# One more quarter by seven products, and the first slice of w_in as float32 through SyncE's queue

## The chip, the cores and the metric

The kernel runs on one NeuronCore of one Trainium2 chip. The metric is the device time of one execution in microseconds (us). The kernel before took 203.43 us in the median of three runs (203.06 to 203.89).

## What is computed

First a linear attention with decay, then a two-layer perceptron with exact GELU on its output. Inputs are float32; q, k and v are [4, 8, 768, 64] (batch, heads, sequence, head width), w_in is [512, 2048] and w_out [2048, 512]; the output is [3072, 512] float32.

```python
for b in range(nb):                       # blocks of 64 positions, S = 768
    intra = (qb @ kb.T) * Dmask[None]     # Dmask: lam ** (i - j) for i >= j, else 0
    out[:, :, sl] = intra @ vb + (qb * lam_pow[None]) @ kv_state
    kv_state = lam_block * kv_state + (kb * rev_pow[None]).T @ vb
x = out.transpose(0, 2, 1, 3).reshape(B * S, H * D)      # [3072, 512]
h = x @ w_in
g = 0.5 * h * (1.0 + erf(h / sqrt(2)))
return g @ w_out
```

## The kernel before

**Tiling.** The sequence is cut into six groups of 128 positions (g = 0 to 5). A group is 128 positions of each of the four batches, so 512 tokens, and is done in two pairs of batches (p = 0, 1). For each group and pair the kernel loads q, k and v, transposes q and k on TensorE (groups 0 to 2) or by DMA (3 to 5), computes scores (`sc` or `u`), masks them on VectorE (`m`), adds to the state (`ka`, `kb`, or within `u` and `ii`), computes the attention output (`o`, `oo`) and writes the scaled result `x` on VectorE. Group 0 goes another way than the rest (`add_paired`, L465): two neighbouring positions lie side by side, scores use four PSUM banks and need four masks, and each scaling of v is one instruction of 128x512.

**The first product** (x times w_in, then GELU) is cut into four quarters of 512 columns of d_ff, c = 0 to 3, in each group. A quarter is computed in one of two ways. The plain one (`add_mm1_half`, L653) has for both pairs two halves H g.j.p with j = 2c and 2c+1, each of 8 matmuls of 128x256 and one GELU on ScalarE: 32 matmuls for a quarter. The other (`add_mm1_quads`, L734) splits the product two by two and uses seven products instead of eight, h g.c.1 to h g.c.7, of 4 matmuls of 128x256 each: 28 matmuls, with two copies (`hm`, `hs`), two adds on VectorE (`ha` L777, `hb` L782) and four GELUs. It needs sums of the slices of x (`X`, once for a group) and of w_in (`V`, once for all groups). STD lists the quarters done the plain way: all of group 0, and quarters 0 and 2 of group 1. The second product (`P`, `add_mm2`) works by seven products throughout, with sums `S` of GELU outputs and `W` of w_out.

**Loads.** q, k, v and both weights are cast from float32 to bfloat16 by the DMA, which GpSimd issues (`nc.gpsimd.dma_start`; L345 for group 0, L356, L317 and L320 for the rest, L369 for w_in, L374 for w_out). w_in comes in four slices of 512 columns: ld.wi0, ld.wi4, ld.wi8, ld.wi12. SyncE's queue carries the load of lam, the DMA transposes and the stores. GpSimd also scales v (`vh`) where the order says so, and it works through its loads and its scalings in one line: a scaling that waits for its v holds up all loads behind it.

**The order.** The instructions of all engines are written out by hand-placed names in the string ORDER (L26 to L76). `Program.emit` prints them in that order, each on its engine; a name may carry another engine behind a slash (`vh000/POOL`). Steps called idleN are dummy matmuls that keep TensorE's clock up; `idleN/SP` means that this one is left out. Costs that stand with the operations are stored and not used when the program is printed. Each engine works strictly in its order, and semaphores are derived from the tiles that an operation reads and writes.

The head of the order, before (cut):

```
ld.wi4 ld.q00 iota ld.k00 ld.v00 tb0 ... ldlam ... ln cols tix tw tpa tid tmp ... Tq00 idle11 Tk00
ld.q01 ld.k01 ld.wi0 xp Ek000/DVE vh001 vh000/POOL ... sc00 ka00 ld.v01 ld.q10 ld.k10 ld.v10 ...
o00 x000 x001 Eq010 Eq011 Ek010 Ek011 H0.0.0a H0.0.0b sc01 idle16 ... H0.3.0a ... vh010/POOL m0101 m0100 m0111
ld.wi8 ld.k11 ld.wi12 vh011 m0110 Tq10 H0.1.0a H0.1.0b ka01 Tk10 kb01 o01 H0.2.0a H0.3.0b H0.2.0b ...
ld.q11 vh101 vh100 ld.v11 Eq100 Eq101 Ek101 Ek100 sa01 ks10 x011 x010 ... u10 sm10 tmk m101 m100 H0.4.0 H0.5.0
```

`ld.q00` is q of group 0 and pair 0; `Tq00` its transpose, `Ek000` the copy of a transposed half from PSUM; `vh000` a scaling of half of v; `H0.0.0a` the first half of the tokens of H0.0.0. Matmuls of all kinds have line L452 in the profile (a helper), transposes L435 and L437, plain copies L300 (ScalarE) and L302 (VectorE).

The functions that the change touches, and what calls them:

Of the kernel before, what the change touches and what calls it, by code (L numbers as in the profile page):

```python
# [26 lines left out]
ld.wi4 ld.q00 iota ld.k00 ld.v00 tb0 idle0/SP ldlam idle1/SP idle2/SP idle3/SP idle4/SP idle5/SP idle6/SP ln cols tix  # L27
tw tpa tid tmp idle7/SP idle8/SP idle9/SP idle10/SP Tq00 idle11 Tk00 ld.q01 ld.k01 ld.wi0 xp Ek000/DVE vh001
vh000/POOL xx xw xc Eq001 Eq000 Ek001 idle12/SP idle13/SP idle14/SP idle15/SP bits sc00 ka00 ld.v01 ld.q10 ld.k10
ld.v10 kb00 m0000 m0011 m0010 m0001 Tq01 Tk01 o00 x000 x001 Eq010 Eq011 Ek010 Ek011 H0.0.0a H0.0.0b sc01 idle16  # L30
idle17/SP idle18/SP idle19/SP idle20/SP idle21/SP idle22/SP idle23/SP H0.3.0a sa00/ACT xv gtab g0.0.0 V0.0 vh010/POOL
m0101 m0100 m0111 ld.wi8 ld.k11 ld.wi12 vh011 m0110 Tq10 H0.1.0a H0.1.0b ka01 Tk10 kb01 o01 H0.2.0a H0.3.0b H0.2.0b
ld.q11 vh101 vh100 ld.v11 Eq100 Eq101 Ek101 Ek100 sa01 ks10 x011 x010 g0.1.0 g0.2.0 u10 sm10 tmk m101 m100
H0.4.0 H0.5.0 i10 g0.4.0 g0.5.0 Tk11 H0.0.1 sa10 Ek110/DVE Ek111/DVE V0.2 V1.0 ks11/DVE g0.3.0 H0.7.0 H0.6.0 g0.0.1
g0.7.0 g0.6.0 H0.2.1 Tq11 o10 Eq110/DVE x101 x100 g0.2.1 Eq111 vh110/ACT H0.1.1 H0.3.1 ld.v20 ld.wo00 ld.k20 vh111 u11
g0.1.1 g0.3.1 sm11 H0.5.1 H0.4.1 V2.1 m111 m110 S0.0.0 V3.0 S1.0.0 V1.2 i11 o11 x110 x111 X0.1 X1.1 vh200/ACT g0.5.1
H1.1.0 H0.6.1 vh201/ACT g1.1.0 g0.4.1 sa11/ACT g0.6.1 H1.0.1 H0.7.1 h1.1.1 H1.0.0 g0.7.1 g1.0.0 g1.0.1 S2.0.0 X2.1
ks20/DVE ld.q21 ld.q20 ld.wo10 Tq20 Tk20 W0.0 S0.0.4 Ek200/DVE Eq201 h1.1.5 hm1.1/DVE Eq200 Ek201/DVE X3.1 W1.0 H1.5.0
H1.4.0 hs1.1 u20 g1.5.0 h1.1.6 h1.1.2 H1.5.1 H1.4.1 m200 m201 sm20 ii20 g1.1.00 g1.5.1 ha1.1 h1.1.3 fe20 g1.4.1 g1.4.0
oo20 h1.1.7 h1.3.5 h1.3.1 H1.1.1 ld.k21 ld.v21 ld.wo01 ld.v31 g1.1.01 vh211/ACT vh210 ld.wo11 ld.q40 ld.k40 V3.2 sa20  # L40
x200 ks21/DVE hb1.1 h1.1.4 P1.0a x201 S1.0.4 g1.1.11 g1.1.10 g1.1.1 P1.0b hs1.3 hm1.3 W0.2 P5.0a P5.0b h1.3.6 h1.3.2
pm.0 ps.0 ld.v30 ld.q30 ld.k30 ld.q31 ld.k31 ld.v40 V2.2 V2.3 S3.0.0 W1.2 W2.2 V2.0 Tq21 S3.0.4 Eq211/DVE ha1.3 Tk21
P6.0a P6.0b h1.3.7 P2.0a g1.3.00 Eq210 W2.0 S0.1.0 hb1.3 Ek210 Ek211 u21 m211 m210 vh300/ACT h1.3.3 P2.0b sm21 h2.0.1
c11.0 vh301/ACT g1.3.01 S2.0.4 pa.0 W3.2 ii21 h1.3.4 fe21 oo21 g1.3.10 g1.3.11 vh310/ACT P3.0a P3.0b P7.0a P7.0b x211
x210 X0.2 X1.2 W3.0 hs2.0 h2.0.2 h2.0.5 c12.0 hm2.0 g2.0.00 sa21/ACT c22.0 S0.1.4 X2.2 h2.0.6 ha2.0 P4.0a P4.0b h2.1.1
Tq30 Tk30 h2.0.7 ks30 S2.1.4 X3.2 hb2.0 h2.0.3 g2.0.01 u30 h2.0.4 P1.1a c21.0/DVE m300 h2.1.5 P5.1a m301 g2.0.10 sm30
vh311 ii30 hs2.1 S1.1.4 fe30/POOL Tq31 st0.11 Tk31 st0.10 Tk40 st0.01 st0.00 Tq40 h2.1.6 P5.1b oo30 hm2.1 ha2.1 h2.1.3
P1.1b h2.1.7 h2.1.2 vh401 sa30/ACT S3.1.4 ks31/DVE x301 x300 u31 pm.1 g2.0.11 hb2.1 h2.1.4 ps.1 S1.1.0 g2.1.01 g2.1.00
h2.2.1 h2.2.5 g2.1.10 m310 S2.1.0 m311 hs2.2 hm2.2/DVE sm31 g2.1.11 P6.1a h2.2.6 P2.1a h2.2.2 ii31 ha2.2 h2.2.7
fe31/POOL oo31 h2.2.3 g2.2.00 hb2.2 sa31/ACT ld.v41 ld.v50 ld.q41 ld.k41 ld.q51 ld.v51 ld.q50 g2.2.01 h2.3.1 h2.2.4  # L50
P2.1b h2.3.5 P6.1b x311 S3.1.0 x310 vh400/DVE hm2.3/DVE g2.2.10 hs2.3 c11.1 ks40 h2.3.6 ha2.3 h2.3.2 u40 h2.3.3 h2.3.7
g2.3.00 X0.3 pa.1 g2.2.11 g2.3.01 m400 X1.3 X2.3 hb2.3 g2.3.11 S2.2.4 m401 sm40/DVE S0.2.4 P3.1a P3.1b h3.0.5 h2.3.4
h3.0.1 P7.1a P7.1b c22.1 hm3.0 g2.3.10 hs3.0 ii40 h3.0.6 ha3.0 c12.1/DVE vh411 X3.3 P4.1a h3.0.2 h3.0.7 h3.0.3
sa40/ACT g3.0.00 g3.0.01 hb3.0 P4.1b h3.1.5 c21.1/DVE S0.2.0 g3.0.11 h3.0.4 h3.1.1 P1.2a g3.0.10 hs3.1 P5.2a h3.1.6
hm3.1 S1.2.4 vh410 S1.2.0 h3.1.2 g3.1.00 st1.01 st1.00 Tk41 Tq41 fe40 st1.11 Tq50 oo40 P5.2b ha3.1 h3.1.7 h3.1.3 x400
hb3.1 x401 S3.2.0 pm.2/DVE ks41 g3.1.01 h3.2.1 P1.2b h3.1.4 h3.2.5 u41 ps.2/DVE P2.2a g3.1.11 g3.1.10 hs3.2 sm41
h3.2.6 hm3.2 m410 m411 P2.2b ii41 h3.2.2 g3.2.00 ha3.2 h3.2.7 hb3.2 fe41/POOL h3.2.3 h3.3.1 oo41 h3.2.4 g3.2.01 h3.3.5
P6.2a g3.2.10 hs3.3 c11.2 hm3.3 g3.2.11 vh500/DVE h3.3.6 P6.2b h3.3.2 vh501 S0.3.0 x410 x411 S3.2.4 ha3.3 h3.3.7 X0.4
pa.2 hb3.3 S1.3.0 X1.4 S3.3.0 S2.2.0 h3.3.3 g3.3.00 P3.2a h3.3.4 h4.0.1 g3.3.11 g3.3.01 h4.0.5 P3.2b P7.2a g3.3.10
hs4.0 h4.0.6 P7.2b h4.0.2 c12.2/DVE X2.4 sa41 hm4.0 ha4.0 X3.4 g4.0.00 h4.0.7 hb4.0 S2.3.4 ks50/DVE c22.2 S0.3.4  # L60
ld.k51 ld.k50 Tk50 st2.00 st1.10 Tq51 Tk51 P1.3a h4.0.3 h4.0.4 h4.1.1 g4.0.01 g4.0.10 h4.1.5 hm4.1 hs4.1 u50 P4.2a
h4.1.6 sm50 h4.1.2 P4.2b g4.1.00 m501 ha4.1 m500 S2.3.0 h4.1.7 h4.2.1 h4.1.3 ks51 g4.0.11 ii50 g4.1.01 hb4.1 S1.3.4
c21.2/DVE vh510 fe50/POOL vh511 h4.1.4 g4.1.10 oo50 hs4.2/DVE h4.2.5 P5.3a x500 x501 hm4.2/DVE P5.3b h4.2.6 u51 ha4.2
h4.2.2 g4.1.11 sm51/DVE h4.2.3 h4.2.7 P1.3b m510 m511 ii51 hb4.2 fe51/POOL st2.10 st2.11 st2.01 g4.2.01 g4.2.00 h4.3.1
pm.3 ps.3/DVE h4.2.4 oo51 g4.2.10 hs4.3 P2.3a h4.3.6 h4.3.5 P6.3a P2.3b g4.2.11 c11.3 x510 x511 hm4.3/DVE ha4.3 h4.3.7
hb4.3 X0.5 h4.3.2 P6.3b S3.3.4 pa.3 g4.3.00 h4.3.3 h4.3.4 h5.0.1 P7.3a P7.3b g4.3.01 g4.3.11 g4.3.10 hs5.0 h5.0.2
h5.0.5 g5.0.00 hm5.0 X1.5 S0.4.4 h5.0.6 X2.5 c22.3 P4.3a P4.3b ha5.0 h5.0.7 h5.0.3 S1.4.4 hb5.0 X3.5 S3.4.4 g5.0.01
P3.3a h5.0.4 h5.1.1 h5.1.5 P3.3b g5.0.10 hs5.1 h5.1.6 hm5.1 g5.0.11 c21.3/DVE S0.4.0 ha5.1 P5.4a h5.1.2 g5.1.00 h5.1.7
S2.4.0 c12.3/DVE hb5.1 S1.4.0 h5.1.3 P5.4b h5.2.1 g5.1.01 h5.1.4 h5.2.5 P1.4a pm.4 g5.1.11 g5.1.10 P1.4b hs5.2/DVE
h5.2.6 hm5.2 ps.4 st3.11 st3.00 st3.10 st3.01 h5.2.2 P6.4a ha5.2 g5.2.00 S0.5.0 h5.2.7 h5.2.3 g5.2.01 hb5.2 P2.4a  # L70
h5.2.4 h5.3.1 P2.4b P6.4b g5.2.11 g5.2.10 c11.4 S0.5.4 S2.4.4 hs5.3/DVE h5.3.6 h5.3.2 h5.3.5 g5.3.00 hm5.3 S1.5.0 pa.4
ha5.3 S3.4.0 P7.4a P7.4b h5.3.7 P3.4a P3.4b S1.5.4 hb5.3 S3.5.0 c22.4 c12.4 h5.3.3 h5.3.4 P4.4a P4.4b S2.5.4 S2.5.0
g5.3.11 g5.3.10 g5.3.01 S0.5.6 S1.5.6 c21.4/DVE S2.5.6 P1.5a P1.5b ps.5 P5.5a P5.5b P6.5a P6.5b pm.5 S3.5.4 st4.01
st4.00 st4.10 st4.11 S3.5.6 pa.5 P2.5a P2.5b c11.5/DVE P7.5a st5.00 P7.5b P3.5a c22.5 P4.5a c12.5a/DVE c21.5a/DVE
P3.5b P4.5b c12.5b c21.5b st5.11 st5.01a st5.10a st5.01b st5.10b
# [66 lines left out]
def kernel(  # L142
# [155 lines left out]
    def copy(eng, dst, src):  # L298
        if eng == "ACT":
            nc.scalar.copy(dst, src)  # L300
        else:
            ENG[eng].tensor_copy(dst, src)  # L302
# [63 lines left out]

    def add_w_in(kf0, kf1):
        f = slice(kf0 * 128, kf1 * 128)
        add("ld.wi%d" % kf0, "POOL", lambda: nc.gpsimd.dma_start(w_in[:, :, f], w_in_r[:, :, f]), (),  # L369
            ["wi%d.%d" % (kf, kh) for kf in range(kf0, kf1) for kh in range(2)], ("w", kf1 - kf0))  # L370

# [625 lines left out]
```

## Time and profile before

| | before |
|---|---|
| median of 3 runs | 203.43 us |
| the profiled execution's own time | 204.17 us |
| span of its instructions | 202.3 us |
| TensorE (PE) busy | 186.3 us, 92% |
| VectorE (DVE) busy | 141.6 us, 70% |
| ScalarE (ACT) busy | 115.4 us, 57% |
| GpSimd (POOL) busy | 82.6 us, 41% |
| mean granted TensorE clock | 0.983 |

How to read it: the time of the profiled execution is the span and 1.87 us around it, and is itself 0.74 us above the median of the runs. In a list of waits a row gives who waited, for what, the sum, the number of waits and the longest. In a timeline a row gives start, duration, engine, line, operation, what was written from what, a count and in brackets the idle time before it with its releaser. In a table of stretches each engine's busy time stands with its count of instructions, then the granted clock, the DMA engines' share and what they moved in GB/s (bytes as written, so for casting loads the bfloat16 bytes). Matmuls are pipelined: a group's busy time, not the mean of one, gives what a matmul costs in a stream.

### The profile page before, as it was taken

How to read it: one execution, taken by the hardware profiler on the slowest of the kernel's cores; microseconds unless marked ns; L12 is line 12 of the kernel's file. 1: busy time of each engine (PE TensorE's matmuls, PEld its weight loads, DVE VectorE, ACT ScalarE, POOL GpSimd, SP SyncE). 2: the span in 40 equal slices, each digit the busy share in tenths (PEclk: the TensorE clock that was granted, in tenths of full speed). 3: DMA queues.
4: the chain of work that ended last, by engine and by line, in shares of the span. 5: the costliest groups of instructions: out<-in, count | busy, mean ns of one | idle time of the engine just before them, and what ended most of it. 6: DMA issues, size and time to landing. Idle time of an engine off the chain costs nothing.

```text
span 202.3 us, 6864 instructions
## 1 busy us (share of the span) xinstructions
PE 186.3 (92%) x2971; PEld 160.0 (79%) x2972; DVE 141.6 (70%) x255; ACT 115.4 (57%) x239; POOL 82.6 (41%) x112
## 2 busy tenths in 40 slices
...
GB/s 53 182 187 174 141 188 159 180 164 166 143 162 151 132 155 190 232 33 21 102 156 214 170 29 52 55 236 26 158 4 0 78 81 52 3 0 104 107 72 139
DMA packets 92398, 23.52 MB, mean 116 GB/s; under 512 B 82128, under 2 KB 92368, under 8 KB 92368
## 3 DMA queue, kind: packets, MB, share of 16 engines
...
q1 hardware_dynamic: 19376, 9.44, 21.0%
...
## 4 chain that ended last, share of the span: by engine, by line
PE 86%; DMA 7%; POOL 3%; DVE 2%; issue 1%; ACT 0%; POOLq 0%; ACTq 0%; DVEq 0%
PE M L452 37%; PE N L452 36%; PE X L452 9%; DMA qr<-in_q_dram 4%; DMA vr<-in_v_dram 3%; PE KV L452 2%; PE N L437 1%; POOL vr L345 1%; PE X L437 1%; POOL qr L345 1%; POOL kr L345 1%; POOL vh L403 1%; POOL w_in L369 0%; DVE N L302 0%; DVE m L782 0%
## 5 line engine op out<-in xcount | busy, mean ns | idle before, releaser
L452 PEld LDWEIGHTS <-w_in 128*128 128x128 bf16 x512 | 47.4, 100 | 7.1 <-issue 0.7
L763 ACT ACTIVATE g<-M 128x512 bf16<-128x512 f32 x51 | 29.7, 596 | 33.1 <-PE M L452 31.7
L452 PE MATMUL M<-x,w_in 128*128 128x256 bf16 (+1 forms) x360 | 45.1, 270 | 1.0 <-DVE x L525 0.9
L452 PEld LDWEIGHTS <-S 128*128 128x128 bf16 x384 | 37.3, 98 | 4.6
L452 PEld LDWEIGHTS <-g 128*128 128x128 bf16 x288 | 28.0, 98 | 3.5
L414 POOL TENSOR_TENSOR vh<-vr,lam_w 128x256 bf16<-128x256 bf16 x16 | 9.9, 663 | 39.5 <-PE X L452 39.4
L452 PE MATMUL N<-w_out,g 128*128 128x256 bf16 x192 | 24.2, 273 | 0.1
L452 PEld LDWEIGHTS <-V 128*128 128x128 bf16 x216 | 20.3, 98 | 2.9 <-issue 0.2
L452 PE MATMUL N<-T,S 128*128 128x256 bf16 x176 | 22.2, 273 | 0.0
L452 PE MATMUL N<-w_out,S 128*128 128x256 bf16 x176 | 21.2, 273 | 0.0
L452 PE MATMUL M<-xs,w_in 128*128 128x256 bf16 x136 | 20.5, 273 | 0.0
L452 PE MATMUL M<-xs,V 128*128 128x256 bf16 x136 | 19.9, 273 | 0.0
L777 DVE TENSOR_TENSOR M<-m,M 128x512 f32<-128x512 f32 x17 | 11.8, 694 | 10.2 <-PE M L452 7.8
L686 DVE TENSOR_TENSOR S<-g 128x1024 bf16<-128x1024 bf16 (+1 forms) x26 | 16.6, 643 | 2.2 <-ACT g L763 2.2
L668 ACT ACTIVATE g<-M 128x512 bf16<-128x512 f32 x24 | 13.8, 595 | 6.4 <-PE M L452 6.3
L782 DVE TENSOR_TENSOR m<-m,M 128x512 f32<-128x512 f32 x17 | 11.6, 685 | 7.8 <-PE M L452 7.6
L588 DVE TENSOR_TENSOR scm<-X,mask 128x512 bf16<-128x512 f32 x20 | 13.1, 685 | 3.4 <-PE KV L452 3.2
L634 DVE TENSOR_TENSOR x<-X,lam_x 128x512 bf16<-128x512 f32 x20 | 13.1, 684 | 1.7 <-PE X L452 1.6
L452 PE MATMUL KV<-vh,kr 64*64 64x64 bf16 x352 | 13.5, 200 | 0.2
L763 ACT ACTIVATE g<-m 128x512 bf16<-128x512 f32 x18 | 11.4, 631 | 3.1 <-DVE m L782 3.1
L356 POOL DMA_DIRECT2D qr<-in_q_dram x10 | 12.0, 1200 | 0.0
L452 PE MATMUL N<-T,g 128*128 128x256 bf16 x96 | 12.0, 273 | 0.0
...
## 6 DMA issues: line engine op xcount, KB each, us to landing
...
```

What stands on the lines that cost most here:

```text
L345: nc.gpsimd.dma_start(to[half(c)].rearrange("i (h e) -> i h e", h=H), bass.AP(src.tensor, src.offset + (2 * p + c) * H * S * D + g * C * D ...
L356: add("ld.%s%d%d%s" % (n, g, p, suffix(cs)), "POOL", lambda: nc.gpsimd.dma_start(dst, source(n, g, p, cs)), (), rkeys(n, g, p, cs), ("load ...
L414: ENG[e].tensor_mul(o_[:, c, h0:h1], v_[:, c, h0:h1], tab[:, h0:h1, None].to_broadcast((128, h1 - h0, D)))
L437: nc.tensor.transpose(b16[:, c], r_[:, c], ident)
L452: return nc.tensor.matmul(*a, skip_group_check=True, **kw)
L588: add(name("m", hi), "DVE", lambda hi=hi: nc.vector.tensor_mul(m_[:, hi, cr], sc[hi][:, cr], mask[:, None, None, :].to_broadcast((128, nc_ ...
L634: add(name("x", bl), "DVE", lambda bl=bl: nc.vector.tensor_mul(x_[:, cr, :, half(bl)], o[bl][:, cr], lam_x[:, None, :, half(bl)].to_broadc ...
L668: lambda: nc.scalar.activation(gt[g % 2][:, 2 * j:2 * j + 2, t], seen(bk, "n t", n=2), ACT.Gelu),
L686: lambda i=i, op=op, l=l, r=r: nc.vector.tensor_tensor(s(i)[0], l[0], r[0], op), l[1] + r[1], s(i)[1],
L763: lambda: nc.scalar.activation(gt[g % 2][:, 4 * c + fo:4 * c + 3 + fo:2, th * 2 * C:(th + 1) * 2 * C], src, ACT.Gelu),
L777: add("ha" + nm, "DVE", lambda: nc.vector.tensor_add(seen(bc, "q t", q=2), f5, seen(bb, "q t", q=2)), [bb, k5], [bc], ("ps", 512))
L782: add("hb" + nm, "DVE", lambda: nc.vector.tensor_add(f7, f5, seen(bb, "q t", q=2)), [bb, k5], [k7], ("ps", 512))
```

## The change

It has three parts. Quarter 2 of group 1's first product leaves STD, so it is done by seven products. The slice ld.wi0 of w_in (columns 0 to 511) is no longer cast by a DMA of GpSimd: SyncE's queue loads it as float32 in two transfers (ld.wi0a, ld.wi0b, half of the rows of w_in each, 512 KB each) into the four output staging tiles `osb`, which hold nothing yet, and four copies of 128x512 (cw00, cw01, cw10, cw11) cast it into the w_in tile, three on ScalarE and one on VectorE. And the whole order is new.

```diff
-STD = ((0, 0), (0, 1), (0, 2), (0, 3), (1, 0), (1, 2))
+STD = ((0, 0), (0, 1), (0, 2), (0, 3), (1, 0))
...
+HWI = (0,)
...
     def add_w_in(kf0, kf1):
         f = slice(kf0 * 128, kf1 * 128)
+        if kf0 in HWI:
+            for kh in range(2):
+                ks = slice(2 * kh, 2 * kh + 2)
+                add("ld.wi%d%s" % (kf0, "ab"[kh]), "SP", lambda ks=ks: nc.sync.dma_start(
+                    osb[:, ks].rearrange("p k z e -> p k (z e)"), w_in_r[:, ks, f]), (),
+                    over(["o%d" % (2 * kh), "o%d" % (2 * kh + 1)]), ("hloadw", 1))
+                for z in range(2):
+                    fz = slice((kf0 + 2 * z) * 128, (kf0 + 2 * z + 2) * 128)
+                    add("cw%d%d" % (kh, z), "ACT|DVE|POOL", lambda e, ks=ks, z=z, fz=fz: copy(
+                        e, w_in[:, ks, fz], osb[:, ks, z, :]), ["o%d.%d" % (2 * kh + k_, z) for k_ in range(2)],
+                        ["wi%d.%d" % (kf0 + 2 * z + y, kh) for y in range(2)], ("cv", 512))
+            return
         add("ld.wi%d" % kf0, "POOL", lambda: nc.gpsimd.dma_start(w_in[:, :, f], w_in_r[:, :, f]), (),
```

The head of the new order (cut):

```
iota ld.q00 ld.wi0a ldlam ln tw tpa tmp ld.k00 cols tb0 tid xp cw01 cw00 ld.wi0b cw10/DVE tix ... ld.v00 ...
idle12 Tq00 bits ... Tk00 idle18 Ek000/DVE Eq001 Eq000 Ek001 sc00 vh000 vh001 ka00 ld.q01 ld.k01
ld.v01 ld.wi4 ld.q10 m0011 m0010 m0000 m0001 Tq01 kb00 Tk01 o00 idle19 ... ld.k10
ld.v10 ld.wi8 vh010/POOL ld.k11 vh011/POOL ld.wi12 xx xw Ek010/DVE x000 cw11 xv xc sa00/ACT Ek011 gtab x001 Eq011/DVE
Eq010/DVE H0.0.0a sc01 H0.1.0a H0.0.0b H0.3.0a m0101 tmk m0111 m0110 m0100 g0.0.0 H0.1.0b Tq10 H0.2.0a V0.0 ka01 kb01
o01 Tk10 H0.2.0b H0.3.0b g0.1.0 sa01/ACT Ek101/DVE x011 Eq100/DVE x010 Eq101/DVE vh100 ks10 Ek100 g0.2.0 H0.5.0 ld.q11
vh101 ld.v11 ld.q20 ld.v20 ld.k20 u10 g0.3.0 sm10 Tk11 H0.4.0 ...
```

Steps whose engine changes up to the scores of group 2's second pair (u21): vh000, vh110, vh201 and vh210 go to VectorE, vh011 from VectorE to GpSimd; Ek010, Eq010, Eq011, Ek101, Eq100, Eq101, hm1.2 and pm.0 are on VectorE in the new order, Ek110, Ek200, Ek201, Eq110, hm1.1, ks11, ks20, ks21, sa01 and sa20 no longer are. Of the dummy matmuls idle12 (two), idle18 and idle19 (one each) are printed; before it was idle11 (two) and idle16 (one). The order of the second half and of the end is new in detail too, with the same steps.

96 lines of the change are left out of this document (47 added, 49 removed).

## Prediction

> **What bounds the kernel now.** I read the page first, then TensorE's waits, then the timeline of the first 30 us, then stretches of it.
>
> ```profile
> span 202.3 us, 6864 instructions
> PE 186.3 (92%) x2971; PEld 160.0 (79%) x2972; DVE 141.6 (70%) x255; ACT 115.4 (57%) x239; POOL 82.6 (41%) x112
> ```
>
> TensorE is busy for 186.3 of 202.3 us, so 16.0 us are left. Its waits say where most of them lie:
>
> ```profile
> PE M L435 <- DMA qr<-in_q_dram: 8.6, 1, 8.6
> PE N L437 <- DMA qr<-in_q_dram: 2.0, 1, 2.0
> PE M L452 <- DVE x L525: 0.9, 1, 0.9
> ```
>
> The first is the wait for the very first load, the second and third come before 22 us, and the stretches show the rest:
>
> ```profile
> 4.00:5.00 1.00, 0.00 (x0) 0.00 (x0) 0.88 (x8) 0.00 (x0) 1.00 (x3) 1.00 1.19 194
> 7.00:8.00 1.00, 0.00 (x0) 0.00 (x0) 0.00 (x0) 1.00 (x5) 1.00 (x2) 1.00 1.79 175
> 19.77:23.18 3.41, 1.40 (x25) 1.34 (x24) 2.75 (x5) 1.41 (x5) 2.84 (x3) 1.00 2.33 146
> 23.00:24.00 1.00, 1.00 (x25) 0.79 (x23) 0.00 (x0) 0.56 (x2) 1.00 (x2) 0.59 0.63 49
> 23.20:30.00 6.80, 6.69 (x147) 5.88 (x144) 2.73 (x6) 3.15 (x6) 6.80 (x10) 0.50 1.47 171
> 29.12:198.89 169.77, 169.50 (x2633) 146.72 (x2632) 126.90 (x219) 100.00 (x205) 58.83 (x78) 1.00 1.01 111
> 198.89:202.30 3.41, 0.00 (x0) 0.00 (x0) 0.00 (x0) 0.37 (x1) 0.00 (x0) 1.00 0.24 80
> ```
>
> From 29.12 to 198.89 us TensorE is busy for 169.50 of 169.77 us. There, only fewer matmuls can help, or an earlier start; the tail of 3.41 us (a copy and the last store) stays. Ahead of 29 us the loads set the pace (175 to 194 GB/s as written), with a hole of half a microsecond or more at 23 us (49 GB/s), and after the thin stretch of 1.40 us of matmuls in 3.41 the granted clock is a half for 6.80 us. So 203 us are about 29 us of start at low yield, 170 us of dense matmuls, and 3.4 us of tail.
>
> **Seven products for quarter 2.** It removes 32 matmuls of 128x256 and adds 28. What one costs in the stream is read from the chain of waits:
>
> ```profile
> 49.97 1.75 PE M L452 x16
> ```
>
> 1.75 / 16 = 0.109 us, so 4 fewer save 0.44 us, and all of that counts, as TensorE is the bound there. It adds two adds and two copies:
>
> ```profile
> L777 DVE TENSOR_TENSOR M<-m,M 128x512 f32<-128x512 f32 x2 | 1.4, 688 | 0.0
> L782 DVE TENSOR_TENSOR m<-m,M 128x512 f32<-128x512 f32 x2 | 1.4, 687 | 1.2 <-PE M L452 1.2
> L300 ACT COPY m<-M 128x512 f32<-128x512 f32 x2 | 1.2, 590 | 1.0 <-PE M L452 1.0
> ```
>
> That is 2 x 0.69 us on VectorE, and with hm1.2 there too 2.07 us, and 0.59 us for hs1.2 on ScalarE. GELUs (four each way) and V sums stay the same in number. What hides it is VectorE's idle time, priced below.
>
> **The slice of w_in by SyncE's queue.** The rows of the start:
>
> ```profile
> 0.74 0.40 SPq L257 DMA_DIRECT2D lam_b<-in_lam_dram  x1
> 1.25 0.94 POOL L369 DMA_DIRECT2D w_in<-in_moe_w_in_dram  x1 [0.80 <-POOLq L981]
> 2.19 1.40 POOL L345 DMA_DIRECT2D qr<-in_q_dram  x2
> 3.32 0.21 ACT L266 ACTIVATE ln<-lam_b 128x8 f32<-128x8 f32 x1 [1.30 <-DMA lam_b<-in_lam_dram]
> 3.63 0.19 POOL L209 IOTA pos<- 128x1 f32 x1
> 3.72 0.29 POOL L210 IOTA row<- 128x128 f32 x1
> 8.57 1.06 PE L435 MATMUL M<-ident,qr 128*64 128x128 bf16 x16 [8.57 <-DMA qr<-in_q_dram]
> 11.57 1.04 POOL L403 TENSOR_TENSOR vh<-vr,lam 128x512 bf16<-128x512 bf16 x1 [1.32 <-DMA vr<-in_v_dram]
> 11.64 0.42 DVE L302 COPY kT<-M 128x512 bf16<-128x512 bf16 x1 [5.61 <-PE M L435]
> 11.98 1.17 DVE L403 TENSOR_TENSOR vh<-vr,lam 128x512 bf16<-128x512 bf16 x1
> 13.21 0.69 DVE L511 TENSOR_TENSOR scm<-X,mask 128x512 bf16<-128x512 f32 x1
> 15.72 0.67 PE L452 MATMUL X<-scm,vh 64*64 64x128 bf16 x32
> 16.46 1.35 DVE L525 TENSOR_TENSOR x<-X,lam_x 128x512 bf16<-128x512 f32 x2 [0.77 <-PE X L452]
> 17.26 1.22 PE L452 MATMUL M<-x,w_in 128*128 128x128 bf16 x16 [0.87 <-DVE x L525]
> 20.34 1.04 POOL L403 TENSOR_TENSOR vh<-vr,lam 128x512 bf16<-128x512 bf16 x1 [2.91 <-DMA vr<-in_v_dram]
> 21.33 0.82 POOL L369 DMA_DIRECT2D w_in<-in_moe_w_in_dram  x1
> 21.83 0.62 PE L437 MATMUL N<-ident,qr 128*128 128x128 bf16 x8 [2.01 <-DMA qr<-in_q_dram]
> 23.32 0.64 PE L452 MATMUL KV<-vh,kr 64*64 64x64 bf16 x16
> ```
>
> Today 512 KB of w_in (ld.wi4, 2.7 us at 194 GB/s) go ahead of q00, which is 256 KB (1.5 us at 175). In the new order ld.wi4 goes behind v01, and what runs ahead of and beside q00 is 1 MB of float32 from SyncE's queue. No load of that kind is in the trace. The nearest row is a stretch of stores, also float32 by SyncE's queue:
>
> ```profile
> 185.50:186.75 1.25, 1.25 (x14) 1.11 (x13) 0.60 (x2) 0.59 (x2) 0.00 (x0) 1.00 1.01 337
> ```
>
> At 337 GB/s it takes 3.1 us, at the 175 of the casting loads 6.0; I take 3.1, for the packets need no cast, and keep 6.0 for the range. So these bytes cost the DMA engines 0.4 us more than ld.wi4 did. They start earlier: SyncE issues at 0.74, and lam's whole way to its reader took 2.58 us (0.74 to 3.32), so I put the first bytes near 1.8, against about 2.9 for GpSimd's (issued at 1.25, and by the same 1.1 to 1.7 us behind). GpSimd itself reaches q00 sooner, at 1.6 instead of 2.19: only the two iotas, 0.3 us, stand ahead of it. In a queue that shares the engines by turns q00 would be complete at 1.8 + 3.1 + 1.5 = 6.4; the same sum before gives 2.9 + 2.7 + 1.5 = 7.1, and TensorE took q00 at 8.57, 1.5 later (slow first packets, and the way from the last packet to the reader). Between 0.7 and 2.0 us sooner, then; I take 1.4, the same for k00 and v00 behind it, with TensorE's first transposes at 7.2. lam now stands behind ld.wi0a and comes about 1.7 us later (ln near 5.0), the identity behind `cols` near 5.9: still ahead of q00. The four casts are 0.59 us each on an engine that waits for transposes then; cover gone, 0.6 us each.
>
> **What is late next.** The lead of 1.4 us shrinks at once. vh000 moves from GpSimd (11.57, beside vh001) to VectorE, where both halves, 1.17 us each, stand ahead of the masks, and the copy Ek010 (0.4 us) stands ahead of x000. So masks that start at 13.21 now would start near 12.8, x000 at about 16.1 instead of 16.46, the first H at 16.9 instead of 17.26; sc01 also waits for two copies on VectorE behind x001 and comes at 18.2 (the two x from 16.1, 1.25 us, two copies of 0.42).
>
> The gain comes behind that. Two stalls of the old order go. TensorE no longer stands before Tq10 (the 2.01 us at 21.83) with H0.1 held up behind it: pieces of H0.0, H0.1 and H0.3, four behind sc01, come ahead of Tq10. And GpSimd issues ld.wi8 before vh010, not behind it; today it idles 2.91 us for v01 until 20.34, issues ld.wi8 at 21.33, and the engines run dry at 23. From 18.2 I add TensorE's work with the granted clock full, by the rows above: sc01 0.6 (32 matmuls, as the outputs at 15.72), four H pieces 2.2 (half of the 1.22 at 17.26, less a tail that the next one covers), Tq10 0.6, H0.2.0a 0.55, ka01 and kb01 1.2, o01 0.7, Tk10 0.6: 24.65; two H pieces more, 25.7. Ahead of u10 stand VectorE's copies and x, from Tk10: three copies of 0.42 and two x of 0.65 make 2.6, from 24.6 to 27.2, and H0.5.0 (8 x 0.109 = 0.9) runs under them. u10, the first scores of group 1, starts at 27.2. Now it starts here:
>
> ```profile
> 26.45 2.74 PE L452 MATMUL M<-x,w_in 128*128 128x128 bf16 x24
> 29.13 0.27 PE L452 MATMUL X<-qT,kT 64*64 64x64 bf16 x4
> ```
>
> That row also shows the clock's price: 24 pieces in 2.74 us are 0.114 each where the 16 at 17.26 took 0.076, so a third of the 6.69 us busy at half clock, 2.2 us, is lost to it. The lead at u10 is 29.13 - 27.2 = 1.9 us, plus 0.9 for H0.5.0, which stood behind u10, plus 0.3 for the rest of the half clock after 29.13: 3.1 us.
>
> **What takes some back.** VectorE:
>
> ```profile
> 17.00:40.00 23.00, 20.46 (x426) 17.84 (x428) 14.12 (x26) 14.11 (x30) 17.56 (x23) 0.85 1.95 167
> 40.00:66.00 26.00, 25.92 (x451) 22.37 (x440) 23.04 (x42) 20.66 (x47) 19.71 (x26) 1.00 1.97 157
> ```
>
> It idles 8.9 us from 17 to 40, and 3.0 from 40 to 66. Counted in the two orders up to u21, VectorE has 86 steps instead of 80: six more, between 0.42 and 0.69 us, about 3.6 us. Running 3.1 us ahead takes that much idle time too, so 6.7 of 11.9 us are spoken for, in an engine that works in strict order. Idle time that lies in the wrong place doesn't count; I let TensorE lose two VectorE steps, 1.3 us, within 0 and 3.1 (the whole lead). The loads keep up: they start 0.7 to 1.4 us earlier and lose the hole at 23 us.
>
> Sum: -3.1 - 0.44 + 1.3 = -2.2 us. The span goes to 200.1, the profiled execution from 204.17 to 202.0, the median, 0.74 lower, to 201.2.
>
> **A rule that speaks against it.** The Trainium skill ("DMA: Bandwidth & Descriptors", Issuing engines are not separate DMA queues) says that transfers from SyncE and GpSimd end up on the same DMA engines and interleave, so that a second issuer saves only the time of issuing. The bytes of 3.1 and 2.7 us above agree: no engine time is saved, 0.4 us is lost.
>
> **Rivals.** *The DMA engines set the pace throughout.* All that group 1's first scores need is the same bytes as before; only the early start (1.1 us), less 0.4, and the hole at 23 (half a microsecond at least) are won. For it: a DMA share of 1.47 to 2.33 up to 66 us. Against: TensorE waits for no load after 22 us. Time: 203.4 - 1.2 - 0.44 and half of VectorE's 1.3 back, as a smaller lead needs less of its idle time: 202.4.
>
> *The clock falls again.* TensorE still waits near 17.5 (x and two copies) and near 27 (copies ahead of u10). If such a stretch is as thin as 19.77 to 23.18, half clock follows, and 2.2 us go: 203.4. For it: fewer than four dummy matmuls. Against: the thin places are about 1 us, not 2.0. The Trainium skill ("TensorE: Matmul & The Clock Gate", Part 1) has the clock decided by windows of about 3.4 us that run freely against the kernel; the 6.80 us here are two of them, and it would make this rival come and go between runs.
>
> *VectorE becomes the bound, slower.* The place is the stretch from 40 to 66 us, where it idles only 3.0: the adds of quarter 2 (2.07), vh110, vh201 and vh210 each stand there ahead of something that TensorE needs soon. If the idle time ahead of 40 us can't be used, since the tiles that these steps read aren't there yet, all 3.6 us fall on TensorE; and if u10 comes no sooner than 28.5, the lead to pay from is 0.6 + 0.9. Then 203.4 - 1.5 - 0.44 + 3.6 = 205.1. It decides once VectorE costs more than 1.9 us. Against: in the old order TensorE waits for VectorE nowhere behind 18 us.
>
> That the change does nothing can be left out for the products (28 for 32 are certain); for the load it is nearly so in itself: the first H waits for x, not for w_in.
>
> **How the numbers follow.** Forecast 201.2, chance 0.5, its own range 199.4 to 202.4; the DMA engines 0.15; the clock 0.18; VectorE 0.17. A measurement here can tell 0.5%, 1.0 us, from no change: faster is below 202.4. That is the forecast almost whole (0.48), half of the DMA case (0.07), and a little of the clock's (0.04): 0.59. Slower is VectorE's case and the 6.0 us load, 0.18; the same 0.23. The range reaches from 199.3, the sum without VectorE's loss (-3.5) and with q00 sooner by 2.0 instead of 1.4, to 204.0, which takes in the clock's case and the milder third of VectorE's, and with them the longer float32 load.
>
> **What would show it.** Right: first transposes near 7.2, the first H near 16.9, u10 near 27.2 with H0.5.0 before it, no wait of TensorE for qr but the first, granted clock 1.0 from 18 us, and waits of TensorE for VectorE of about a microsecond between 40 and 70. Wrong: transposes later than 8.5 (a slow float32 load), a half clock after 20 us, or a TensorE waiting for `ha`, `hb`, `vh` or S by more than 3 us.

## The result and the profile after

The kernel after takes 205.51 us in the median of 4 runs (205.26 to 205.97); the kernel before, with one run more, 203.25 (202.77 to 203.89). The ratio is 1.0112, with a 95% interval of 1.0077 to 1.0147: slower by 2.3 us, where 2.2 us less was forecast. The profiled execution of after took 205.42 us, its span is 203.7, and the mean granted clock is 0.992. The profiled executions of two experiments (e6 and e11 below) ran far slower than their other runs, in 632.78 and 380.01 us, and aren't used.

From the page of after:

```profile
span 203.7 us, 6903 instructions
PE 186.8 (92%) x2971; PEld 158.5 (78%) x2971; DVE 144.4 (71%) x264; ACT 118.8 (58%) x250; POOL 79.0 (39%) x105
...
osb<-in_moe_w_in_dram SPq DMA_DIRECT2D x2, 512.0 KB, 5.9
```

TensorE's busy time hardly moved (186.3 before). The last row is the float32 slice: 5.9 us from issue to landing is the median of its two halves, which took 4.8 and 6.9 us; the second, issued at 1.76, landed near 8.7. TensorE's waits in after:

```profile
PE M L891 <- DVE idle L261: 7.8, 1, 7.8
PE M L466 <- DMA w_in<-in_moe_w_in_dram: 1.7, 1, 1.7
PE X L466 <- DVE qT L304: 0.6, 1, 0.6
PE N L451 <- DMA qr<-in_q_dram: 0.6, 1, 0.6
PE M L466 <- DVE x L539: 0.5, 1, 0.5
PE N L466 <- ACT osb L302: 0.5, 1, 0.5
```

The 2.0 us ahead of Tq10 shrank to 0.6, where the forecast had no wait left, but there is a new 1.7 us for w_in and a wait for a copy at the very end. (The first row is idle1, two dummy matmuls, which is printed in the new order beside those named above.) The timeline of after, with the steps that the prediction dated:

```profile
0.74 0.46 SPq L374 DMA_DIRECT2D osb<-in_moe_w_in_dram  x1
1.26 0.45 SPq L259 DMA_DIRECT2D lam_b<-in_lam_dram  x1
1.38 1.55 POOL L347 DMA_DIRECT2D qr<-in_q_dram  x2 [0.22 <-issue]
6.77 0.21 ACT L268 ACTIVATE ln<-lam_b 128x8 f32<-128x8 f32 x1 [4.75 <-DMA lam_b<-in_lam_dram]
9.41 1.40 POOL L347 DMA_DIRECT2D kr<-in_k_dram  x2 [2.40 <-DMA qr<-in_q_dram]
9.98 1.06 PE L449 MATMUL M<-ident,qr 128*64 128x128 bf16 x16 [0.31 <-DMA qr<-in_q_dram]
18.24 0.61 PE L466 MATMUL M<-x,w_in 128*128 128x128 bf16 x8 [0.54 <-DVE x L539]
28.16 1.05 PE L466 MATMUL M<-x,w_in 128*128 128x256 bf16 x8 [1.70 <-DMA w_in<-in_moe_w_in_dram]
29.13 0.22 PE L466 MATMUL X<-qT,kT 64*64 64x64 bf16 x4
```

GpSimd issues q00 0.8 us sooner than before (1.38 for 2.19), yet TensorE takes it 1.4 us later (9.98 for 8.57). GpSimd's issuing of k01 waits 2.40 us until q00 is there, and everything behind it in GpSimd's line with it. Stretches of the start, after first and then before (the last two columns are the DMA engines' share and GB/s):

```profile
2.00:3.00 1.00, 0.00 (x0) 0.00 (x0) 0.51 (x4) 0.02 (x1) 1.00 (x3) 1.00 0.77 225
4.00:5.00 1.00, 0.00 (x0) 0.00 (x0) 0.00 (x0) 0.00 (x0) 1.00 (x3) 1.00 0.40 93
5.00:6.00 1.00, 0.00 (x0) 0.00 (x0) 0.00 (x0) 0.00 (x0) 1.00 (x2) 1.00 0.17 50
2.00:8.00 6.00, 0.22 (x1) 0.13 (x2) 1.35 (x8) 1.23 (x3) 5.00 (x8) 1.00 0.75 189
```

```profile
2.00:8.00 6.00, 0.00 (x0) 0.00 (x0) 2.31 (x15) 2.90 (x9) 5.95 (x11) 1.00 1.11 137
```

From 2 to 8 us after moves 6 x 189 = 1134 kB, but 1049 of these are the float32 megabyte: of bytes that become bfloat16 tiles it is 85 + 524 = 609, against 6 x 137 = 822 before. From 4 to 6 us, with q00 long issued, the engines move little.

The rest of the difference, in stretches from the start of u10 to that of the step P1.5a, and from there to TensorE's last matmul, and the half clock of after:

```profile
29.13:187.05 157.92, 157.43 (x2510) 135.53 (x2509) 123.14 (x211) 100.58 (x209) 57.81 (x74) 0.99 1.06 112
187.05:200.16 13.11, 12.61 (x114) 10.84 (x111) 6.01 (x12) 2.02 (x4) 0.00 (x0) 1.00 0.23 77
29.81:33.22 3.41, 3.41 (x50) 2.59 (x49) 1.98 (x3) 2.27 (x4) 3.41 (x5) 0.50 2.11 170
```

```profile
29.12:186.42 157.30, 157.05 (x2522) 135.87 (x2522) 121.82 (x209) 98.48 (x202) 58.83 (x78) 1.00 1.07 110
186.42:198.89 12.47, 12.45 (x114) 10.85 (x111) 5.08 (x11) 1.53 (x3) 0.00 (x0) 1.00 0.37 124
```

So the spans differ by 0.0 us at u10, 0.62 in the dense stretch, 0.64 at the end, and 0.1 behind the last matmul: 1.4 us, as 203.7 - 202.3. (By the medians it is 2.3; the profiled execution of before was 0.9 us above its median, with 6.8 us at half clock ahead of 30 us.) The half clock of after isn't the cause: its other three runs had a mean granted clock of 0.997 to 1.000 and took 205.26 to 205.97 us.

### The profile page after: what moved, and what is told of

It is laid out like the page before. It is cut to its first block, busy times and chain, and to the rows that moved or that the text cites. A ratio compares the mean times of both kernels' runs of the same rounds, so it can differ in the third digit from the quotient of the medians.

```text
span 203.7 us, 6903 instructions
## 1 busy us (share of the span) xinstructions
PE 186.8 (92%) x2971; PEld 158.5 (78%) x2971; DVE 144.4 (71%) x264; ACT 118.8 (58%) x250; POOL 79.0 (39%) x105
## 3 DMA queue, kind: packets, MB, share of 16 engines
q0 software_dynamic: 72464, 13.11, 81.7%
## 4 chain that ended last, share of the span: by engine, by line
PE 80%; DMA 10%; POOL 4%; DVE 3%; issue 1%; ACT 0%; DVEq 0%; POOLq 0%; ACTq 0%
PE M L466 35%; PE N L466 35%; PE X L466 8%; DMA w_in<-in_moe_w_in_dram 6%; DMA qr<-in_q_dram 4%; PE KV L466 1%; PE X L451 1%; PE N L451 1%; POOL kr L347 1%; POOL vr L347 1%; DVE x L648 1%; DVE scm L602 1%; DVE xs L729 1%; POOL qr L358 1%; POOL kr L358 1%
## 5 line engine op out<-in xcount | busy, mean ns | idle before, releaser
L466 PEld LDWEIGHTS <-w_in 128*128 128x128 bf16 x496 | 44.6, 98 | 9.0 <-DMA w_in<-in_moe_w_in_dram 1.9
L466 PE MATMUL M<-x,w_in 128*128 128x256 bf16 (+1 forms) x336 | 42.6, 266 | 2.4 <-DMA w_in<-in_moe_w_in_dram 1.7
L466 PEld LDWEIGHTS <-V 128*128 128x128 bf16 x228 | 21.9, 98 | 3.1 <-issue 0.3
L466 PE MATMUL N<-w_out,S 128*128 128x256 bf16 x176 | 22.0, 273 | 0.0
L466 PE MATMUL M<-xs,w_in 128*128 128x256 bf16 x144 | 21.6, 273 | 0.1
L466 PE MATMUL M<-xs,V 128*128 128x256 bf16 x144 | 20.5, 273 | 0.0
L791 DVE TENSOR_TENSOR M<-m,M 128x512 f32<-128x512 f32 x18 | 12.5, 695 | 6.8 <-ACT m L302 3.2
L796 DVE TENSOR_TENSOR m<-m,M 128x512 f32<-128x512 f32 x18 | 12.3, 685 | 5.2 <-PE M L466 4.9
L777 ACT ACTIVATE g<-m 128x512 bf16<-128x512 f32 x19 | 11.9, 629 | 1.5 <-DVE m L796 1.5
L302 ACT COPY osb<-N 128x512 f32<-128x512 f32 (+1 forms) x12 | 6.6, 551 | 10.3 <-PE N L466 10.2
```

The lines of the kernel that those rows point to most:

```text
L466: return nc.tensor.matmul(*a, skip_group_check=True, **kw)
L777: lambda: nc.scalar.activation(gt[g % 2][:, 4 * c + fo:4 * c + 3 + fo:2, th * 2 * C:(th + 1) * 2 * C], src, ACT.Gelu),
L791: add("ha" + nm, "DVE", lambda: nc.vector.tensor_add(seen(bc, "q t", q=2), f5, seen(bb, "q t", q=2)), [bb, k5], [bc], ("ps", 512))
L796: add("hb" + nm, "DVE", lambda: nc.vector.tensor_add(f7, f5, seen(bb, "q t", q=2)), [bb, k5], [k7], ("ps", 512))
```

## The experiments

Theory 1, at first: the float32 load holds back the loads that TensorE waits for, and without it the forecast gain appears. Its rival: the DMA engines set the pace to about 45 us whatever comes first, so an early start is worth nothing. The last four kernels (e13 to e16) then part the load itself (theory A) from the place of lam behind it (theory B). Each ratio is to the kernel before, run beside it, with its interval. Intervals are 0.2 to 0.6% either way, so steps of 0.3 to 0.4% between two kernels are weak by themselves.

**The end of the order alone (e4).** The last steps of after as they stood before:

```diff
-... P2.5b P3.5a P7.5a st4.10 c12.5a/DVE c11.5/DVE P7.5b c22.5 P3.5b P4.5a c21.5a
-c12.5b/DVE st5.01a st5.00 st5.11 st5.10a st5.01b P4.5b c21.5b st5.10b
+... P2.5b st4.10 c11.5/DVE P7.5a st5.00 P7.5b P3.5a c22.5 P4.5a c12.5a/DVE c21.5a/DVE
+P3.5b P4.5b c12.5b c21.5b st5.11 st5.01a st5.10a st5.01b st5.10b
```

> The changed kernel with the end of the order as before (the last product's halves in the order P3.5a, P4.5a, P3.5b, P4.5b, with the copy of P4.5a on VectorE under P3.5b). In the changed kernel P4.5b stands 0.66 us behind the copy of P4.5a. If that wait counts in full: lower by 0.5 to 0.7 us (204.9). If the stores at the end are later anyway: within 0.2 us.

Measured: 204.26 us, 1.0069 (1.0041 to 1.0097). The end of after, and the same stretch of this kernel:

```profile
198.71 0.37 ACT L302 COPY osb<-N 128x256 f32<-128x256 f32 x1 [9.09 <-PE N L466]
199.13 1.03 PE L466 MATMUL N<-T,g 128*128 128x256 bf16 x8 [0.50 <-ACT osb L302]
```

```profile
187.92:200.38 12.46, 12.45 (x114) 10.85 (x111) 6.10 (x12) 2.02 (x4) 0.00 (x0) 1.00 0.26 86
```

In after P4.5b writes the accumulator of P4.5a again and so stands behind its copy; before, P3.5b lay between. 13.11 us go back to 12.46: 0.65 us are the end's, and by the ratios 0.43%.

**The slice cast by GpSimd, at three places.** The new order without float32: first of all with the old end (e5), behind k01 (e1), and behind k01 with the old end (e15).

```diff
-HWI = (0,)
+HWI = ()
-iota ld.q00 ld.wi0a ldlam ... xp cw01 cw00 ld.wi0b cw10/DVE tix
+ld.wi0 iota ld.q00 ldlam ... xp tix          (e5; in e1 and e15: ... ld.q01 ld.k01 ld.wi0)
```

> The new order with the slice of w_in cast by a DMA of GpSimd and issued ahead of everything (as the kernel before does with its first slice), no copies, and the end of the order as before. Theory 1 (the start hangs on how many bytes the DMA engines have moved; a 512 KB slice first, issued in 0.94 us for 2.7 us of transfer, is a backlog that hides GpSimd's issuing, and float32 through SyncE lost it): loads up to wi8 complete no later than before (v10 by 24.0, wi8 by 26.9), u10 at 28.5 or sooner with H0.5.0 done, P1.5a near 185, time 201.0 to 202.3. Rival (the new order is worse in itself): 204 or more.

> The changed kernel with the slice of w_in loaded as before, cast by a DMA of GpSimd (one transfer, placed behind k01), and without the four copies; order otherwise the new one. Theory 1 (the float32 load and lam behind it hold the DMA engines at the start, so q00 and all loads behind it come 1.2 us later than before): the first transposes start at 7.0 us or sooner instead of 9.98, u10 before 28, and the time falls by 1.5 to 3 us against the changed kernel, to 202.5 to 204.0. Rival (the new order itself, with H0.5.0 ahead of u10 and more steps on VectorE, is what costs): within 0.5 us of the changed kernel's 205.5.

> The new order with the old end, no float32, the slice cast by GpSimd behind k01 instead of ahead of q00. Theory A (what counts is how many bytes are moved in the first 8 us; this kernel moves fewer than the one with the slice first): 204.0 to 204.6 us, ratio 1.005 to 1.008. Theory B (the place of the slice is nothing as long as lam comes early): 203.3 to 203.8, ratio 1.001 to 1.004.

Measured: e5 203.12 us, 1.0030 (0.9999 to 1.0061); e1 204.71, 1.0078 (1.0045 to 1.0112); e15 203.73, 1.0045 (1.0024 to 1.0067). The timeline and the stretch from 2 to 8 us, first of e5, then of e1:

```profile
8.47 1.07 PE L449 MATMUL M<-ident,qr 128*64 128x128 bf16 x16 [1.85 <-DMA qr<-in_q_dram]
27.99 0.22 PE L466 MATMUL X<-qT,kT 64*64 64x64 bf16 x4
```

```profile
2.00:8.00 6.00, 1.89 (x4) 0.43 (x4) 2.60 (x16) 2.01 (x5) 5.92 (x12) 1.00 1.13 139
```

```profile
6.12 1.06 PE L449 MATMUL M<-ident,qr 128*64 128x128 bf16 x16
28.86 1.05 PE L466 MATMUL M<-x,w_in 128*128 128x256 bf16 x8 [1.82 <-DMA w_in<-in_moe_w_in_dram]
29.84 0.22 PE L466 MATMUL X<-qT,kT 64*64 64x64 bf16 x4
```

```profile
2.00:8.00 6.00, 3.42 (x21) 1.36 (x21) 1.82 (x10) 2.78 (x7) 6.00 (x10) 1.00 1.19 112
```

Theory 1 is half right, and e1's time lies between the two forecasts. Without float32 q00 comes at 6.12, sooner than forecast, but u10 comes later than in e5, which started 2.4 us behind: H0.5.0 waits for w_in. GpSimd's small loads take it 0.68 us each to issue, its slices 0.78 to 0.94 for four times the bytes, so a slice first fills the engines (139 GB/s for 112) while it issues the rest. And even e5, with no float32 and the old end, isn't faster than before. Loads don't explain that by themselves: behind q00, TensorE in e5 waits for no load, but 1.8 us for x, 1.0 for a GELU and 0.6 for a copy.

**A slice behind v01 in the old order, no other edit (e2).**

```diff
-ld.wi4 ld.q00 iota ld.k00 ...  sc00 ka00 ld.v01 ld.q10
+ld.q00 iota ld.k00 ...         sc00 ka00 ld.v01 ld.wi4 ld.q10
```

> The kernel before with one thing moved: the load of columns 512 to 1023 of w_in, first in GpSimd's line, goes behind v01. It asks whether a start lead reaches the end. If the dense stretch begins sooner by as much as q00 comes sooner: q00 2.7 us earlier, first transposes near 6.0, time lower by 1.0 to 2.0 us (201.3 to 202.3). If the scores of group 1 hang on the sum of all bytes ahead of them, which is the same: within 0.4 us of 203.3.

Measured: 206.02 us, 1.0131 (1.0085 to 1.0177).

```profile
5.99 1.06 PE L435 MATMUL M<-ident,qr 128*64 128x128 bf16 x16 [5.99 <-DVE mask L226]
20.40 0.62 PE L452 MATMUL M<-x,w_in 128*128 128x128 bf16 x8 [1.75 <-DMA w_in<-in_moe_w_in_dram]
29.59 0.22 PE L452 MATMUL X<-qT,kT 64*64 64x64 bf16 x4 [0.22 <-DVE idx L243]
```

A start 2.6 us sooner (5.99 for 8.57) ends 2.7 us later. This speaks for the rival: the lead of q00 on which the forecast built isn't worth anything here. Two things weaken it. The 1.75 us are the wait of H0.3.0a for the very slice that was moved, so the run also shows the price of that slice coming later. And all four runs had a low granted clock (0.966 to 0.983); the profiled execution of before, at 0.983 too, took 1.7 us less than that of e2, not 2.7.

**The float32 load alone, in the old order**, with lam behind its first half (e7, as in after) and with lam first (e13). The branch of `add_w_in` is put into before, with HWI = (4,) and the four casts on VectorE.

```diff
-ld.wi4 ld.q00 iota ... ldlam ...
+ld.wi4a ld.q00 iota ... ldlam ld.wi4b ... cw00/DVE cw01/DVE cw10/DVE cw11/DVE   (e7)
+ldlam ld.q00 iota ld.wi4a ... ld.wi4b ... cw00/DVE cw01/DVE cw10/DVE cw11/DVE   (e13)
```

> The kernel before with one thing changed: its first slice (columns 512 to 1023) goes as float32 through SyncE's queue, half of it ahead of lam, half behind, with four copies on VectorE. It has the float32 load alone, in the old order. If that load is the loss: q00 complete at 9 us or later instead of 8.0, first transposes near 9.8, later loads 0.7 to 1.2 us late, time higher by 1 to 2.5 us (204.3 to 205.8). If the loss needs the new order: within 0.5 us of 203.3, or lower, as GpSimd issues q00 0.9 us sooner.

> The old order with its first slice as float32 by SyncE's queue, as in the run of that alone (1.0078 of before), but lam is loaded ahead of it. Theory A (the 1 MB of float32 keeps q, k and v from the DMA engines, that is the price): still 204.0 to 204.6 us, ratio 1.005 to 1.008, q00 taken near 10. Theory B (the price is lam behind the float32 load, which makes ln and all that hangs on it 3.4 us later): 203.0 to 203.5, ratio 1.000 to 1.002, with q00 taken as late as under A.

Measured: e7 204.21 us, 1.0078 (1.0043 to 1.0113); e13 203.68, 1.0047 (1.0026 to 1.0067). In e7 q00 is taken at 10.57, in e13 at 10.30. So the load with its four copies, against the same slice cast by GpSimd, costs 0.5%, 0.9 us, and 0.3% more where lam stands behind it, though there the intervals overlap; neither theory A nor B of that expectation holds alone, it is some of each. From e7:

```profile
10.57 1.07 PE L448 MATMUL M<-ident,qr 128*64 128x128 bf16 x16 [10.57 <-DMA qr<-in_q_dram]
28.03 0.22 PE L465 MATMUL X<-qT,kT 64*64 64x64 bf16 x4 [0.22 <-DVE idx L244]
34.06 2.79 PE L465 MATMUL M<-x,w_in 128*128 128x256 bf16 x24 [0.92 <-DMA w_in<-in_moe_w_in_dram]
```

Here u10 comes 1.1 us sooner than before, as the clock stays full (before lost 2.2 us to it), and P1.5a starts at 186.16 for 186.42: of the lead 0.3 is left.

**lam ahead of the float32 load in the new order**, with the end of after (e3) and with the old end (e14):

```diff
-iota ld.q00 ld.wi0a ldlam ln
+iota ld.q00 ldlam ld.wi0a ln
```

> The changed kernel with lam's load ahead of the float32 slice in SyncE's queue. If it is lam's 128 small packets between the two halves of the slice that leave the engines idle from 4.5 to 5.5 us and hold q00: ln at 3.5 instead of 6.77, q00 complete by 7.5 instead of 9.2, first transposes near 8, time lower by about 1 us (204.5). If the float32 bytes themselves are what q00 waits for: ln early, but q00 complete at 8.5 or later and the time within 0.5 us of the changed kernel's.

> The kernel after with the end of the order as before and lam ahead of the float32 slice, so both single edits together. Theory A: lam's place adds nothing, so as the end alone, 204.3 us, ratio 1.005 to 1.008. Theory B: the two add up, 203.4 to 203.8, ratio 1.001 to 1.004, as where GpSimd casts the slice first of all.

Measured: e3 204.74 us, 1.0075 (1.0049 to 1.0101); e14 204.21, 1.0067 (1.0036 to 1.0098). e14 equals the end alone (1.0069), while e3 is 0.4% below after, with overlapping intervals; what lam's place is worth in the new order stays open. The time of e3 is near its first forecast (204.5), but not for the reason given there, which was q00 by 7.5: q00 is still taken at 9.91. What does go is the hole. From e3:

```profile
4.00:5.00 1.00, 0.66 (x2) 0.28 (x3) 0.56 (x2) 0.99 (x2) 1.00 (x3) 1.00 1.00 225
5.00:6.00 1.00, 1.00 (x3) 0.15 (x1) 0.00 (x0) 0.34 (x2) 1.00 (x2) 1.00 0.97 272
6.00:7.00 1.00, 0.23 (x1) 0.00 (x0) 0.00 (x0) 0.42 (x1) 1.00 (x2) 1.00 1.15 361
```

Where after moves 93 and 50 GB/s (4 to 6 us), e3 moves 225 and 272, and 361 behind that. By queue, SyncE's moves 0.62 MB from 3 to 6 us and 0.33 MB from 6 to 7; GpSimd's, with q00 issued long before, moves nothing from 3 to 6 and 0.03 MB from 6 to 7. So the megabyte takes about 4.5 us here: it begins slowly and ends near the 337 GB/s of the stores, and q00 still comes behind nearly all of it.

**lam held back in the old order, no float32 (e16).**

```diff
+        add("lgate", "POOL", lambda: nc.gpsimd.memset(lam_b, 1.0), (), ["lam_b"], ("t", 100))
...
-ld.wi4 ld.q00 iota ld.k00 ... ln cols tix tw tpa tid tmp
+ld.wi4 ld.q00 iota lgate ld.k00 ... ln tix tw tpa tid tmp cols
```

> The kernel before, with nothing changed but that lam's load is held until GpSimd has issued q00 and made its tables, so that ln comes near 6.8 us instead of 3.3 (VectorE's steps that need ln stand behind those that don't). No float32. Theory A: 203.0 to 203.4 us, ratio 0.998 to 1.002, as masks and x need lam only from 11 us on. Theory B: 204.0 to 204.6, ratio 1.005 to 1.008.

Measured: 207.73 us, 1.0219 (1.0177 to 1.0262), far past both. The load of lam, 4 KB, issued at 4.08 among GpSimd's loads, takes 7.4 us:

```profile
4.08 0.39 SPq L258 DMA_DIRECT2D lam_b<-in_lam_dram  x1
11.51 0.21 ACT L267 ACTIVATE ln<-lam_b 128x8 f32<-128x8 f32 x1 [9.49 <-DMA lam_b<-in_lam_dram]
12.02 1.06 PE L436 MATMUL M<-ident,qr 128*64 128x128 bf16 x16 [12.02 <-DMA qr<-in_q_dram]
```

```profile
8.00:9.00 1.00, 0.00 (x0) 0.00 (x0) 0.00 (x0) 0.00 (x0) 0.74 (x2) 1.00 0.45 43
9.00:10.00 1.00, 0.00 (x0) 0.00 (x0) 0.00 (x0) 0.00 (x0) 0.00 (x0) 1.00 1.08 99
```

While its packets of 32 bytes are under way, the engines move 43 and 99 GB/s where before moves 179 and 175, and TensorE takes q00 3.4 us later (12.02 for 8.57); GpSimd's line, too, stands 3.43 us for q00. So it isn't only that ln is late, as theory B had it: while lam's packets are under way, the loads that TensorE waits for move at a quarter to a half of their rate. Lam's packets don't fill the engines then: from 8 to 9 us the engines' share falls to 0.45, from 1.82 in before. Why is not shown. In after lam's packets lie in the empty stretch from 4 to 6 us.

**The float32 load held back**, by its place in the order and a read of v00 (e9), and by a write of VectorE into the staging tiles once v00 is there (e10); lam first in both.

```diff
-iota ld.q00 ld.wi0a ldlam ... xp cw01 cw00 ld.wi0b cw10/DVE tix ... sc00 vh000
+iota ld.q00 ldlam ... xp tix ... ld.v00 ld.wi0a ld.wi0b                   (e9)
+iota ld.q00 ldlam ... xp tix ... sc00 gate ld.wi0a ld.wi0b vh000          (e10)
+    add("gate", "DVE", gate, rkeys("v", 0, 0), over(["o%d" % i for i in range(4)]), ("t", 140))
```

> The changed kernel with both halves of the float32 slice held back until v of group 0, pair 0 has landed (SyncE waits for it), lam first, and the four copies on ScalarE further on. It asks whether float32 through SyncE is slow and shuts GpSimd's queue out in itself, or only at the start. If in itself: from about 10 us GpSimd's loads stand still for 4 to 5 us and the 1 MB takes 5 us again. If only at the start (the first reads): 1 MB in 3.1 to 4 us while GpSimd's loads go on at a part of their rate; q00 complete near 5.0, first transposes near 6.5. Time 204 to 206 either way, as the first H then waits for the copies.

> The changed kernel with lam first and the float32 slice really held back: two one-column copies of v into its staging tiles, on VectorE, that SyncE's transfers must wait for, so that they are issued once v of group 0, pair 0 has landed; the casts follow on ScalarE, ahead of the first H. If float32 through SyncE is slow and crowds GpSimd's loads in itself: 1 MB takes 5 us again from about 10, q01 and its followers late, time 204.5 or more. If only the start is slow: q00 complete near 5.0, transposes at 6.2, 1 MB in 3 to 4 us beside GpSimd's loads, and the time below the 204.74 of lam first.

Measured: e9 204.96 us, 1.0094 (1.0062 to 1.0125); e10 209.1, 1.0324 (1.0269 to 1.0379). In e9 a read made no wait, and the load still went at the start: it tells only that later casts bring nothing. In e10 it was held:

```profile
9.68 0.91 SPq L378 DMA_DIRECT2D osb<-in_moe_w_in_dram  x2
17.08 1.14 ACT L302 CAST w_in<-osb 128x512 bf16<-128x512 f32 x2 [5.32 <-DMA osb<-in_moe_w_in_dram]
19.62 1.14 ACT L302 CAST w_in<-osb 128x512 bf16<-128x512 f32 x2 [1.40 <-DMA osb<-in_moe_w_in_dram]
```

```profile
12.00:18.00 6.00, 3.96 (x80) 2.81 (x76) 3.86 (x8) 0.92 (x2) 5.37 (x6) 1.00 1.26 269
```

The megabyte needs until 19 us although nothing small stands between. From 12 to 18 us 269 GB/s flow, 1.6 MB, of which about 1 MB is float32 and 0.6 GpSimd's loads, where those alone reach 177 to 193 (before, 9 to 18 us). So here the two queues do share, and the load takes 6 us for its part (1.03 MB from 13 to 19 us); together they don't reach the 337 GB/s of the stores.

**Quarter 2 plain again, on e5's order (e6)** (hand-placed H1.4 and H1.5, about where they stood before):

```diff
-STD = ((0, 0), (0, 1), (0, 2), (0, 3), (1, 0))
+STD = ((0, 0), (0, 1), (0, 2), (0, 3), (1, 0), (1, 2))
```

> The kernel of the run before this in the list with quarter 2 of group 1 the plain way again (32 matmuls for 28, its halves and GELUs placed by hand where the seven products stood). If the four matmuls count in full and the four steps more on VectorE and ScalarE are hidden: slower by 0.4 to 0.9 us than with seven products (the upper end for hand placing). If VectorE's adds cost what the matmuls save: equal within 0.3 us.

Measured: 204.58 us, 1.0081 (1.0054 to 1.0108), over e5 by 1.0 us by the ratios and 1.46 by the medians. Four matmuls are 0.44; the rest may be the placing, which this run can't separate. So it gives no sign that the seven products slow after, and no price for them either.

**Two moves of one step.** ld.wi8 ahead of vh010 in the old order (e11), and H0.5.0 behind u10 in e5 (e12):

```diff
-V0.0 vh010/POOL m0101 m0100 m0111 ld.wi8     Ek100 g0.2.0 H0.5.0 ld.q11 ... u10
+V0.0 ld.wi8 vh010/POOL m0101 m0100 m0111     Ek100 g0.2.0 ld.q11 ... u10 H0.5.0
```

> The kernel before with one load moved: ld.wi8 is issued ahead of GpSimd's scaling vh010, which waits for v01, so the DMA engines no longer run dry at 23 us. If the loads set the pace from there on: wi8 complete 0.9 us sooner and the time 0.4 to 0.9 lower than before. If TensorE's stalls there come from the order of its own work and the clock: within 0.3 us of before.

> The new order with the cast slice first and the old end (203.12 in the median), and H0.5.0 moved from ahead of u10 to behind it, as in the order before. H0.5.0 waits for wi8, u10 for v of group 1, issued just before wi8. If the wait for wi8 ahead of u10 is what keeps this order from beating the old one: 0.4 to 0.9 us lower, 202.2 to 202.7. If both come at nearly the same time: within 0.3 us.

Measured: e11 202.73 us, 0.9999 (0.9959 to 1.0039); e12 203.10, 1.0015 (0.9983 to 1.0048). Neither filling the hole at 23 us nor an earlier u10 (26.13 in e12) shows a gain. But the interval of e11 still allows 0.8 us less, nearly all of the 0.4 to 0.9 that was expected of loads that set the pace, so that case isn't ruled out there. No version here beats the kernel before.

## Why the prediction was wrong

**The step that failed: "I take 3.1, for the packets need no cast".** In after the bytes of the megabyte fill 6 us, 2 to 8, the other end that was kept for the range. Two of these are nearly empty, with lam's small packets between its halves; without them it takes about 4.5 us (e3), as the load begins slowly, and beside GpSimd's loads 6 (e10). So q00 came 1.4 us later, not 1.4 sooner: 9.98 for the 7.2 forecast. The text had named its own sign of this ("transposes later than 8.5"). The nearest row was one of stores, which run the other way; a load's price wasn't in the trace, and the likeliest case was built on one end of it. "A queue that shares the engines by turns" failed as well, as GpSimd's queue moved three packets from 2 to 6 us in after, but for q00 it changes nothing: the sum had put q00 behind the whole megabyte already. And the sum gives 6.4 + 1.5 = 7.9, 0.7 us sooner than 8.57; the 1.4 that was taken has no term of its own.

**The step beneath it, that an early q00 is a lead to be kept, failed by itself.** e1, e2 and e15 have q00 at about 6 us and gain nothing; e2 loses 2.7. "The loads keep up" was wrong there: TensorE waits 1.8 to 2.7 us for w_in between 20 and 32 us, and in e1 and e15 0.3 and 0.6 for x near 38. The rival "the DMA engines set the pace throughout" comes nearest as a mechanism; "throughout" is too much, as e5 shows. Its time, 202.4, was wrong as it still let the start come early.

**The clock, and the execution that the forecast started from.** By the prediction's own price, 2.2 us of the lead of 3.1 at u10 are the half clock in the profiled execution of before (granted clock 0.983). Of the 94 executions of the kernel before that ran beside the experiments, 79 had a mean granted clock of 0.993 or more, and their median is 202.78 us; that of the other 15 is 203.98. So most executions of before had little of this loss to win back: the profiled 204.17 lies 1.4 us above that first median, and the 0.74 us taken off covers half of it. In after the fall came as that rival said, behind the 1.70 us for w_in, and costs 1.6 us: from u10 to H0.6.0 after needs 4.53 us, e4 at full clock 2.93. But it came in one of four runs, and the runs without it are as slow.

**The Trainium skill's rule** ("DMA: Bandwidth & Descriptors", Issuing engines are not separate DMA queues), that a second issuer saves only issuing, fits: e13 loads the same slice through a second queue, with twice the bytes written, and is 0.47% slower. The Trainium skill ("DMA: Bandwidth & Descriptors", Queues, rings and completion order) has the engines alternate between queues by packets. In e10 both queues progress side by side (1.01 MB of float32 and 0.59 MB by GpSimd's queue from 12 to 18 us); at the start of after and e3 they don't, and in e16 the engines' share falls while both queues have work, so turns alone don't explain these runs.

**Stalls of the old order.** Tq10 waits 0.6 instead of 2.0 us. From a first H that is 0.98 us late (18.24 for 17.26) the new order makes up for that and for H0.5.0 (0.9) by 29.13, but that is no more than the clock: before ran at half clock from 23.2 to there. At full clock nothing of it is left: the old order with the float32 load and lam first (e13, q00 at 10.30) has u10 at 27.77, and with 0.87 for H0.5.0 at 28.64; the new order with both (e14, q00 at 9.78) has it at 28.61. With a start as early as before, as in e5, u10 comes at 27.99; forecast was 27.2.

**What takes back.** VectorE was priced at 1.3 us and as a rival at 3.6. TensorE waits for VectorE nowhere behind 40 us in after. Against before, the dense stretch of e4's profiled execution (156.04 us from 31.88 to 187.92) does without H0.5.0 (0.87) and the rest of the half clock (0.88 us at half speed, 0.4): 157.30 - 1.3 = 156.0. So the 0.44 of seven products don't show: about as much is lost, well under 1.3. It is the difference of two orders in one execution each, and no run names where.

**Left out altogether: the end.** "With the same steps" was taken for "at the same cost"; its new order costs 0.65 us.

The sum: of 1.12%, the end is 0.43; with the old end, the float32 slice against one cast by GpSimd is 0.2 to 0.4 in the new order (e4 and e14 at 1.0069 and 1.0067, e15 and e5 at 1.0045 and 1.0030) and 0.5 to 0.8 in the old; the remaining 0.30 to 0.45, where the interval of e5 just includes no change and that of e15 doesn't, is the new order with its seven products, which gained nothing. With intervals of 0.2 to 0.4% these shares are a best account, not a measurement of each. Open are why the float32 load begins so slowly, why GpSimd's queue got so little beside it at the start and its part in e10, where else the new order loses, and what the seven products are worth alone.
